# Attention with beacons and a low-rank mixer on one core: two q loads on another queue, a weight quarter ahead of half of v, and small loads issued sooner

## The chip, the core and the metric

The kernel runs on one core of a Trainium2 chip. The metric is the device time of one execution in microseconds (us); lower is better. The core has five engines that run side by side and wait for one another through semaphores: TensorE (PE, matrix products and transposes), VectorE (DVE), ScalarE (ACT), GpSimd (POOL) and SyncE (SP). In the profile PE's weight loads have a line of their own, PEld. DMAs are issued by POOL (the software queue, q0 in the profile; it can convert f32 to f16 on the way) or by SP and ACT (hardware queues, which here move f32 as f32).

## The reference

```python
# q, k, v: (B=8, H=8, S=576, D=64); beacon_k, beacon_v: (8, 8, 16, 64); all f32
k_all, v_all = concat([beacon_k, k]), concat([beacon_v, v])      # 592 keys
scores = q @ k_all.T / 8, causal over the 576 tokens, beacons always seen
x = softmax(scores) @ v_all            # laid out as (B, S, H * D = 512)
h = x.transpose @ U @ V                # U: (576, 32), V: (32, 576)
u = x + h.transpose
out = u + relu(u @ w_ch1) @ w_ch2      # 512 -> 2048 -> 512
```

## The kernel before, in words

Work goes in *pairs*: two heads of one batch at a time, four pairs to a batch, 32 in all. For a pair, PE transposes q and k (`qkT_units`, lines 277 and 283) into PSUM, DVE copies them to `qT` and `kT` (line 310), PE makes the scores (`score_units`, line 350, with the causal mask added on PE at line 342 for pairs 0, 1 and 4), ACT takes the exponentials (line 356), DVE masks them where PE did not (`mask_head`, lines 326 and 328), and PE multiplies by v (`av_unit`, line 399), after which DVE normalises into `xb` (lines 407 and 408). When a batch is done the low-rank product follows (for the first batch `first_mix`: `head` at line 491 needs `Usb`, `rest` at line 508 needs `Vsb`), and then the two large products in blocks of 512 tokens (`mlp_units`, lines 536 and 562), whose units are played between the later pairs' steps. All of it stands in an order written out by hand: each engine executes its own instructions strictly in that order.

The change touches the opening, up to about 20 us, in which batch 0 goes through attention with no large product to lie beside it. Its loads are:

- `load_first` brings q and k of pair 0 (`stq`, `stk`, f32) by SP and ACT. `build_masks` adds q of pair 1 by SP, into the second part of `stq`, and k of pair 1 by POOL. A cell of `stq` is zeroed on DVE first (line 126); the DMA waits for that, which places it behind the memset in time.
- For pairs 2 and 3, POOL loads k and q, converted to f16, into `Ls[0]` (line 205). `by_heads` transposes such a tile head by head, 12 transposes a pair. A pair that came in f32 is first copied to an f16 tile with both heads beside each other (`regroup`, line 270), and `in_pair` then needs 6 transposes.
- v of batch 0 comes in two halves, heads 0 to 3 (`HALVES[0]`) and heads 4 to 7 (`HALVES[1]`), five DMAs each (`v_tokens`, line 220), by POOL. Pairs 0 and 1 use the first half, pairs 2 and 3 the second.
- `emit_w1(i)` loads a quarter of w_ch1 (line 191), by POOL; its first quarter is first used by line 536, after pair 3's products have begun.
- `small_loads` zeroes a cell of its tile on DVE (line 167), issues U and V by SP (lines 169 to 174) and returns `cast`, which rounds them on POOL to `Usb` and `Vsb` (lines 178 and 179) and then spreads copies by SP (lines 183 and 184).

POOL issues its DMAs in order, one after the other, and each takes it some time. PSUM has eight banks, handed out in a fixed rotation (`pst`, `emptying`).

Of the kernel before, what the change touches and what calls it, by code (L numbers as in the profile page):

```python
# [11 lines left out]
F32 = mybir.dt.float32  # L12
# [6 lines left out]
P = 128  # L19
# [11 lines left out]
def kernel(  # L31
# [13 lines left out]
    nc = tc.nc  # L45
    B, H, S, D = q.shape
# [18 lines left out]
    TJ = 6  # L65
# [29 lines left out]
    gtp = ctx.enter_context(tc.tile_pool(name="gtp", bufs=2))  # L95
# [9 lines left out]
    def pst(shape, dtype, name):  # L105

        b = emptied.pop(0)
        t = psum.tile(shape, dtype, tag=f"bank{b}", name=name)
        bank_of[id(t)] = (b, t)
        return t  # L110

    def emptying(t):
        emptied.append(bank_of.pop(id(t))[0])
# [8 lines left out]
    def build_masks():  # L122
        make_identity(nc, ident)
        nc.vector.memset(bigmask[:, 0, P - Nb : P], F16_MAX)
        nc.vector.tensor_copy(out=identb, in_=ident)
        nc.vector.memset(first[1][0:1, 2, 0:1], 0.0)
        token_load(nc.sync, q[0], first[1], SETS[1])
        make_upper_triangular(nc, mask, val=F16_MAX, diag=True)
        token_load(nc.gpsimd, k[0], Ls[0][0][0], SETS[1])
        nc.vector.tensor_copy(out=bigmask[:, 0, 0 : P - Nb], in_=mask[:, Nb:P])  # L130
        nc.vector.tensor_copy(out=bigmask[:, 1, :], in_=mask)
        for i in range(2):
            nc.vector.tensor_scalar(
                out=negmask[:, i, :], in0=bigmask[:, i, :], scalar1=1.0, scalar2=NEG,
                op0=ALU.is_lt, op1=ALU.mult,
            )
        prs[0] = [None, regroup(first, 0, 1, V, act_copy)]
# [26 lines left out]
    def small_loads():  # L164

        f = utp.tile([P, NT * R + S], F32, name="small", tag="ut")
        nc.vector.memset(f[0:1, 0:1], 0.0)
        uf, vf = f[:, 0 : NT * R].rearrange("p (j r) -> p j r", r=R), f[0:R, NT * R :]
        nc.sync.dma_start(out=uf[: nq[0], 0, :], in_=moe_U[0 : nq[0], :])
        nc.sync.dma_start(  # L170
            out=uf[:, 1 : NT - 1, :], in_=moe_U[q0[1] : QM, :].rearrange("(j p) r -> p j r", p=P)
        )
        nc.sync.dma_start(out=uf[:NL, NT - 1, :], in_=moe_U[QM:S, :])
        nc.sync.dma_start(out=vf, in_=moe_V)

        def cast():
            for rr, jj in ((nq[0], slice(0, 1)), (P, slice(1, NT - 1)), (NL, slice(NT - 1, NT))):
                nc.gpsimd.tensor_copy(out=Usb[:rr, jj, :], in_=uf[:rr, jj, :])
            nc.gpsimd.tensor_copy(out=Vsb[0:R, :], in_=vf)
            for cc in range(NCC):  # L180
                rs = ds(R * cc, R)
                if cc:
                    nc.sync.dma_start(out=Vsb[rs, :], in_=Vsb[0:R, :])
                nc.sync.dma_start(out=Vend[rs, cc, :], in_=Vsb[0:R, QM:S])

        return cast

    def emit_w1(i):
        w1r = moe_w_ch1.rearrange("(cc p) f -> p cc f", p=P)
        fs = ds(FF // 4 * i, FF // 4)  # L190
        nc.gpsimd.dma_start(out=w1[:, :, fs], in_=w1r[:, :, fs])
# [9 lines left out]
    def beacon_load(eng, src, dst, hs):  # L201
        eng.dma_start(out=dst[0:Nb], in_=src[hs].rearrange("h p d -> p h d"))  # L202

    def token_load(eng, src, dst, hs):
        eng.dma_start(out=dst[0:TP, hs, :], in_=src[hs].rearrange("h (p j) d -> p h (j d)", j=TJ))  # L205

    def key_beacons(eng, src, dst, hs):
        beacon_load(eng, src, dst[TP:TB, hs, (TJ - 1) * D : TJ * D], hs)

    def by_head(vs):  # L210
        return vs[:, :].rearrange("p (c h e) -> p c h e", h=H, e=E)

    def v_beacon(bsrc, vs):
        beacon_load(nc.gpsimd, bsrc, by_head(vs)[:, 0, :, 0:D], ALLH)

    def v_tokens(src, vs, hs, js=range(NT)):
        dst = by_head(vs)[:, :, hs, 0:D]
        for j in js:
            a = Nb if j == 0 else 0
            nc.gpsimd.dma_start(  # L220
                out=dst[a : a + nq[j], j, :, :], in_=src[hs, ds(q0[j], nq[j]), :].rearrange("h p d -> p h d")
            )
# [5 lines left out]
    def by_token(t):  # L228
        return t.rearrange("p h (j d) -> p j h d", j=TJ)
# [3 lines left out]
    def qk_tiles():  # L233

        t = [stage.tile([P, TJ * DM], F16, name=f"st{i}", tag=f"st{i}") for i in range(2)]
        st = [x[:, :].rearrange("p (h e) -> p h e", h=H) for x in t]
        whole = [x[:, 0 : NT * DM].rearrange("p (j h d) -> p j h d", h=H, d=D) for x in t]
        return st, whole
# [8 lines left out]
    def keep_warm(ps, n, a=ident):  # L247


        w = ps.shape[-1] // P  # L250
        for _ in range(n):
            nc.tensor.matmul(
                ps[:, 0 : w * P].rearrange("p (a b) -> p a b", b=P), a,
                a.rearrange("p (a b) -> p a b", a=1).broadcast_to([P, w, P]),
                start=True, stop=True,
            )

    def idle(n, a):
        ps = pst([P, 512], F32, name="idle")
        keep_warm(ps, n, a)  # L260
        emptying(ps)

    def regroup(st, c, i, *copies, beacons=True):

        t = pairs.tile([P, TJ, 2, D], F16, name=f"pr{i}", tag=f"pr{i}")
        src = by_token(st[i][:, 2 * c : 2 * c + 2, :])
        w = TJ // len(copies)
        for a, copy in enumerate(copies):
            js = slice(w * a, w * (a + 1))
            copy(out=t[0:TP, js], in_=src[0:TP, js])  # L270
        if i == 0 and beacons:
            copies[0](out=t[TP:TB, TJ - 1], in_=src[TP:TB, TJ - 1])
        return t
# [359 lines left out]
    Ls, qTs, xbs = {}, {}, {}  # L633
# [35 lines left out]
    SETS = [slice(2 * c, 2 * c + 2) for c in range(NH2)]  # L669

    first = []

    def load_first():

        kf = gtp.tile([P, 2, TJ * D], F32, name="stk", tag="gT")
        qf = gtp.tile([P, 4, TJ * D], F32, name="stq", tag="gT")
        first.extend([kf, qf])
        for src, dst in ((q[0], qf), (k[0], kf)):
            for eng, h in ((nc.sync, 0), (nc.scalar, 1)):
                token_load(eng, src, dst, slice(h, h + 1))  # L680
        Ls[0] = qk_tiles()
        key_beacons(nc.gpsimd, beacon_k[0], Ls[0][0][0], ALLH)
        nc.scalar.activation(out=warm, in_=ones, func=AF.Exp)

    def act_copy(out, in_):
        nc.scalar.activation(out=out, in_=in_, func=AF.Copy)

    prs = {}
    V = nc.vector.tensor_copy
# [32 lines left out]
    def scores_of(p):  # L722
        b, c = divmod(p, NH2)
        return score_units(c, qTs[b], kTs[b % 2], expts_of(p), p in ON_PE)
# [86 lines left out]

    with tc.manual_schedule(engines={ENG.PE, ENG.Activation, ENG.DVE, ENG.SP, ENG.Pool}):
        load_first()
        build_masks()
        for c in (2, 3):
            for src, dst in zip((k[0], q[0]), Ls[0][0]):
                token_load(nc.gpsimd, src, dst, SETS[c])
            if c == 2:
                v_beacon(beacon_v[0], vss[0])
                v_tokens(v[0], vss[0], HALVES[0])  # L820
        prs[0][0] = regroup(first, 0, 0, V, act_copy, beacons=False)
        idle(IDLE[0], plain)
        t0, sc = qkT_of(0), scores_of(0)
        t0[0]()
        idle(IDLE[4], ident)
        t0[1]()
        sc[0](IDLE[1], gs=[1, 0])
        prs[1] = [None, regroup(first, 1, 1, V)]
        for u in qkT_of(1):
            u()  # L830
        clear()
        cast = small_loads()
        sc[1]([3, 2], False)
        sc = scores_of(1)
        sc[0](IDLE[2])

        v_tokens(v[0], vss[0], HALVES[1])
        emit_w1(0)
        cast()
        Ls[1] = qk_tiles()  # L840
        (kt, qt), _ = Ls[1]
        token_load(nc.gpsimd, k[1], kt, HALVES[0])
        token_load(nc.gpsimd, q[1], qt, HALVES[0])
        key_beacons(nc.gpsimd, beacon_k[1], kt, ALLH)
        emit_w1(1)
        token_load(nc.gpsimd, k[1], kt, HALVES[1])
        token_load(nc.gpsimd, q[1], qt, HALVES[1])
# [7 lines left out]
        for p in range(2):  # L855
            qt, kt = qkT_of(p + 2)
            kt()
            sc[1]([3, 2], False)
            qt()
            av = av_of(p)  # L860
            av[0]()
            mask_head = sc[3]
            sc = scores_of(p + 2)
            if p:
                mask_head(0)
            sc[0](0, av[1])
            if p:
                mask_head(1)
# [122 lines left out]
        for p in range(NP1, NP):  # L991
            b, c = divmod(p, NH2)
# [128 lines left out]
```

## Time and profile before

| | |
|---|---|
| median of 3 runs | 351.5 us (350.47, 351.5, 351.79) |
| profiled execution, its own time | 349.7 us |
| its span in the trace | 348.0 us |
| PE busy | 341.3 us of it |
| DVE, ACT, POOL busy | 189.7, 163.6, 97.8 us |
| POOL's DMA queue | 18.18 MB in 87440 packets |
| hardware queue q1 | 22.84 MB in 58928 packets |
| granted TensorE clock | 0.998 |

A timeline row gives the start in us, the time until the last instruction of the row ends, the engine (a "q" behind it stands for the engine's sequencer, which issues a DMA), the line, the operation, output<-inputs, the count, and in brackets the idle time of the engine before it with what ended it. A row of DMA issues gives the count, the size written, and the us from the start of the issue to the landing.

### The profile page before, as it was taken

What the parts mean: (1) busy time and instruction counts of PE and PEld (TensorE: products, weight loads), DVE (VectorE), ACT (ScalarE), POOL (GpSimd) and SP (SyncE); (2) the same over time, 40 slices, a digit from 0 to 9 for tenths busy, and PEclk for the clock granted to TensorE, in tenths of its full rate; (3) what the DMA queues carried; (4) which work ended last, traced back from release to release, by engine and by line L of the source; (5) the groups of instructions that cost most, each with busy time, mean ns of one, the idle gap of its engine ahead of it and who ended that gap; (6) DMA issues with size and microseconds to landing.
All of it is one profiled execution on the core that took longest, in us unless ns stands there. A gap on an engine that the chain in (4) does not pass through costs nothing.

```text
span 348.0 us, 7791 instructions
## 1 busy us (share of the span) xinstructions
PE 341.3 (98%) x3084; PEld 173.2 (50%) x3084; DVE 189.7 (55%) x493; ACT 163.6 (47%) x358; POOL 97.8 (28%) x137
## 2 busy tenths in 40 slices
PE   8899999999999999999999999999999999999995
PEld 4565565455554455444554445455445444444443
DVE  6676965788875553554465556535655542323311
ACT  6957851578723664167615752494434203202300
POOL 8966714544506457303930130000000000000000
PEclk9999999999999999999999999999999999999999
DMA  9999999999999999991999697713122314013011
GB/s 166 135 186 170 169 200 171 216 148 154 128 142 145 167 133 132 154 213 14 146 139 237 64 117 123 184 38 68 62 75 47 69 62 121 2 60 106 17 66 64
DMA packets 146635, 41.88 MB, mean 120 GB/s; under 512 B 131488, under 2 KB 142080, under 8 KB 146592
## 3 DMA queue, kind: packets, MB, share of 16 engines
q0 software_dynamic: 87440, 18.18, 68.2%
q1 hardware_dynamic: 58928, 22.84, 36.0%
q8 instruction: 26, 0.43, 0.5%
q10 hardware_dynamic: 224, 0.30, 0.2%
q14 instruction: 17, 0.14, 0.1%
HBM read 37.37 MB, written 9.44 MB: 134 GB/s over the span
## 4 chain that ended last, share of the span: by engine, by line
PE 93%; POOL 2%; DMA 2%; issue 1%; DVE 1%; ACT 1%; POOLq 0%
PE gps L536 36%; PE cps L562 35%; PE po L399 8%; PE sps L384 6%; DMA st<-in_q_dram 2%; PE tps L277 1%; PE sps L350 1%; POOL vs L220 1%; PE cph L588 1%; PE qtp L436 1%; POOL st L205 1%; PE tps L283 1%; PE ups L461 1%; PE ups L415 1%; ACT expt L356 0%
## 5 line engine op out<-in xcount | busy, mean ns | idle before, releaser
L536 PE MATMUL gps<-uT,w 128*128 128x512 f16 x576 | 136.0, 379 | 0.1
L562 PE MATMUL cps<-w,gT 128*128 128x512 f16 x560 | 130.9, 379 | 0.0
L390 ACT ACTIVATE expt<-sps 128x496 f16<-128x496 f32 x192 | 82.5, 534 | 71.5 <-PE sps L384 71.5
L549 ACT ACTIVATE gT<-gps 128x512 f16<-128x512 f32 x86 | 50.9, 622 | 78.8 <-PE gps L536 78.6
L536 PEld LDWEIGHTS <-w 128*128 128x128 f16 x576 | 51.8, 98 | 58.0 <-issue 2.4
L562 PEld LDWEIGHTS <-gT 128*128 128x128 f16 x560 | 50.8, 98 | 58.9 <-issue 6.2
L551 DVE TENSOR_SCALAR gT<-gps 128x512 f16<-128x512 f32 x58 | 40.0, 690 | 41.9 <-PE gps L536 40.5
L575 DVE TENSOR_TENSOR ob<-cps,ut 128x512 f32<-128x512 f32 x31 | 21.4, 691 | 48.3 <-PE cps L562 47.5
L220 POOL DMA_DIRECT2D vs<-in_v_dram x50 | 39.6, 810 | 17.1 <-PE gps L536 5.8
L399 PEld LDWEIGHTS <-expt 128*128 128x128 f16 (+1 forms) x960 | 36.2, 98 | 12.7 <-issue 0.8
L399 PE MATMUL po<-vs,expt 128*128 128x65 f16 (+1 forms) x960 | 38.9, 194 | 0.0
L408 DVE TENSOR_TENSOR xb<-po,rec 128x320 f16<-128x320 f32 x64 | 31.5, 492 | 2.2
L326 DVE TENSOR_TENSOR expt<-expt,bigmask 128x512 f16<-128x512 f16 x58 | 24.1, 416 | 6.7 <-ACT expt L390 6.7
L356 ACT ACTIVATE expt<-sps 128x496 f16<-128x496 f32 (+2 forms) x64 | 27.1, 584 | 0.9 <-PE sps L350 0.8
L407 DVE RECIPROCAL rec<-po 128x5 f32<-128x5 f32 x64 | 12.1, 188 | 27.0 <-PE po L399 26.8
L384 PE MATMUL sps<-qT,kT 64*128 64x80 f16 (+4 forms) x288 | 23.3, 281 | 0.1
L202 POOL DMA_DIRECT2D vs<-in_beacon_v_dram x8 | 4.3, 536 | 57.8 <-PE po L399 57.7
L384 PEld LDWEIGHTS <-kT 64*128 64x128 f16 x288 | 9.9, 94 | 18.3 <-issue 14.8
L651 POOL DMA_DIRECT2D st<-in_q_dram x20 | 16.9, 863 | 6.6 <-DMA vs<-in_v_dram 2.7
L651 POOL DMA_DIRECT2D st<-in_k_dram x20 | 17.0, 883 | 3.4 <-DMA st<-in_q_dram 3.4
L448 DVE TENSOR_TENSOR uT<-ups,uT 128x496 f16<-128x496 f32 x24 | 14.5, 667 | 5.0 <-PE ups L461 5.0
L310 DVE COPY qT<-tps 128x576 f16<-128x576 f16 (+1 forms) x16 | 11.8, 736 | 4.6 <-PE tps L283 2.8
(98 smaller groups left out, 161.9 us busy)
## 6 DMA issues: line engine op xcount, KB each, us to landing
out_dram<-ob SPq DMA_DIRECT2D x35, 256.0 KB, 2.3
vs<-in_v_dram POOLq DMA_DIRECT2D x18, 128.0 KB, 6.9
w<-in_moe_w_ch_dram POOLq DMA_DIRECT2D x4, 512.0 KB, 6.1
w<-in_moe_w_ch_dram POOLq DMA_DIRECT2D x2, 1024.0 KB, 13.6
st<-in_k_dram POOLq DMA_DIRECT2D x12, 128.0 KB, 8.6
st<-in_q_dram POOLq DMA_DIRECT2D x12, 128.0 KB, 9.6
st<-in_k_dram POOLq DMA_DIRECT2D x2, 576.0 KB, 13.2
st<-in_q_dram POOLq DMA_DIRECT2D x2, 576.0 KB, 16.1
```

The lines of the kernel that those rows point to most:

```text
L220: nc.gpsimd.dma_start(out=dst[a : a + nq[j], j, :, :], in_=src[hs, ds(q0[j], nq[j]), :].rearrange("h p d -> p h d"))
L326: nc.vector.tensor_tensor(out=e4, in0=e4, in1=bigmask, op=ALU.min)
L356: nc.scalar.activation(out=ex[i][:, ds(SLOT * g, gw[g])], in_=ps[g, i][:, 0 : gw[g]], func=AF.Exp, scale=scale)
L384: nc.tensor.matmul(ps[p, g, i][:, ds(o, w)], kT[hp, c, ds(P * ch, P)], qT[hp, c, ds(qa, w)], start=True, stop=True,)
L390: nc.scalar.activation(out=at[p][3][i][:, ds(SLOT * g, gw[g])], in_=ps[p, g, i][:, 0 : gw[g]], func=AF.Exp, scale=scale)
L399: nc.tensor.matmul(po[:, j, :], ex[0 : nk[c], ds(blk[(c, j)], P)], vs[0 : nk[c], ds(c * H * E + h * E, E)], start=(c == 0), stop=(c == j),)
L408: nc.vector.tensor_tensor(out=xb[:, :, ds(h * D, D)], in0=po[:, :, 0:D], in1=r.broadcast_to([P, NT, D]), op=ALU.mult)
L536: nc.tensor.matmul(g[:, 0:n], w1[:, cc, ts(dc, P)], uT[:, cc, ds(t0, n)], start=(cc == 0), stop=(cc == NCC - 1))
L549: nc.scalar.activation(out=gT["t"][:, dc, 0:n], in_=g[:, 0:n], func=AF.Relu)
L551: nc.vector.tensor_scalar_max(out=gT["t"][:, dc, 0:n], in0=g[:, 0:n], scalar1=0.0)
L562: nc.tensor.matmul(ps[:m, :], gT["t"][:, dc, ds(P * i, m)], w2[:, dc, :], start=(dc == 0), stop=turned and dc == NDC - 1, skip_group_check ...
L651: nc.gpsimd.dma_start(out=dst[a : m[j], j, :, :], in_=src[:, ds(q0[j], nq[j]), :].rearrange("h p d -> p h d"))
```

## The change

- q of pairs 2 and 3 comes by SP, in f32, into `stq`, which grows from four heads to eight. `load_q` zeroes the cells on DVE and issues the loads; for pair 1 this is what was there before, for pairs 2 and 3 it stands behind pair 0's `regroup`. DVE casts each of the two q's to f16 (`regroup`): pair 2's behind `clear()`, pair 3's behind the copy of pair 2's k. Their transposes are the 6 of `in_pair` instead of the 12 of `by_heads`.
- POOL no longer issues these two q loads.
- `small_loads` (U and V by SP) is called behind pair 0's first scores instead of behind `clear()`.
- w_ch1's first quarter is issued ahead of v's second half instead of behind it.
- `cast` stands behind the first k, q and beacon loads of batch 1 instead of ahead of them.

```diff
 def build_masks():
...
-        nc.vector.memset(first[1][0:1, 2, 0:1], 0.0)
-        token_load(nc.sync, q[0], first[1], SETS[1])
+        load_q(1)
...
-        qf = gtp.tile([P, 4, TJ * D], F32, name="stq", tag="gT")
+        qf = gtp.tile([P, H, TJ * D], F32, name="stq", tag="gT")
...
+    def load_q(*cs):
+        for c in cs:
+            nc.vector.memset(first[1][0:1, 2 * c, 0:1], 0.0)
+        for c in cs:
+            token_load(nc.sync, q[0], first[1], SETS[c])
...
         for c in (2, 3):
-            for src, dst in zip((k[0], q[0]), Ls[0][0]):
-                token_load(nc.gpsimd, src, dst, SETS[c])
+            token_load(nc.gpsimd, k[0], Ls[0][0][0], SETS[c])
             if c == 2:
                 v_beacon(beacon_v[0], vss[0])
                 v_tokens(v[0], vss[0], HALVES[0])
         prs[0][0] = regroup(first, 0, 0, V, act_copy, beacons=False)
+        load_q(2, 3)
...
         sc[0](IDLE[1], gs=[1, 0])
+        cast = small_loads()
         prs[1] = [None, regroup(first, 1, 1, V)]
         for u in qkT_of(1):
             u()
         clear()
-        cast = small_loads()
+        prs[2] = [None, regroup(first, 2, 1, V)]
         sc[1]([3, 2], False)
         sc = scores_of(1)
         sc[0](IDLE[2])
 
+        emit_w1(0)
         v_tokens(v[0], vss[0], HALVES[1])
-        emit_w1(0)
-        cast()
         Ls[1] = qk_tiles()
         (kt, qt), _ = Ls[1]
         token_load(nc.gpsimd, k[1], kt, HALVES[0])
         token_load(nc.gpsimd, q[1], qt, HALVES[0])
         key_beacons(nc.gpsimd, beacon_k[1], kt, ALLH)
+        cast()
         emit_w1(1)
...
             kt()
+            if p == 0:
+                prs[3] = [None, regroup(first, 3, 1, V)]
             sc[1]([3, 2], False)
             qt()
```

## The prediction

> **What bounds the kernel now.** The first view is the page's busy times, the second the waits of PE over the whole span.
>
> ```profile
> PE 341.3 (98%) x3084; PEld 173.2 (50%) x3084; DVE 189.7 (55%) x493; ACT 163.6 (47%) x358; POOL 97.8 (28%) x137
> ```
>
> ```profile
> PE sps L350 <- DVE qT L310: 0.6, 2, 0.3
> PE tps L283 <- DMA st<-in_q_dram: 0.4, 1, 0.4
> ```
>
> PE is busy for 341.3 of 348.0 us, and of its few waits only one is for a transfer: a transpose that waits 0.4 us for q. So whatever the change gives or takes must show as PE idle time in the opening, and what PE gains there it keeps only if no later wait takes its place. The third view, the chain that ended last, shows where that wait lies. It is pair 3's q.
>
> ```profile
> 9.82 5.47 DMA st<-in_q_dram
> 15.29 0.04 issue
> 15.34 0.47 PE tps L283 x12
> 15.80 0.02 issue
> 15.82 0.77 DVE qT L310
> 16.59 0.05 issue
> 16.64 0.58 PE sps L350 x4
> 17.22 0.57 PE po L399 x15
> 17.78 0.41 PE sps L350 x8
> 18.19 0.56 PE po L399 x15
> ```
>
> The load is issued at 9.82 and lands at 15.29. PE transposes it, DVE copies it, pair 3's first scores start at 16.64, and from there one piece of PE work follows the other without a gap: pair 1's second head, pair 3's last scores, and at 18.19 the first head of pair 2 times v, which ends at 18.75. The timeline of ACT, the fourth view, shows the same delay from the other side.
>
> ```profile
> 6.88 9.95 ACT L356 ACTIVATE expt<-sps 128x464 f16<-128x464 f32 x24 [0.62 <-PE sps L350]
> 17.05 3.39 ACT L356 ACTIVATE expt<-sps 128x496 f16<-128x496 f32 x8 [0.23 <-PE sps L350]
> ```
>
> Pairs 0 to 2 keep ACT occupied without a break from 6.88 to 16.83; then it stands for 0.23 us until pair 3's scores come. So up to 16.6 ACT sets the pace, and small delays on PE before that are covered. The stage's limit is ACT first, then q's landing, then PE.
>
> **Pair 3's q sooner: -0.44 us.** By SP the load is issued behind DVE's cast of pair 0's k, so soon after 5.35. How long such a load takes is seen in SP's timeline and in the DMA issues: q of pair 1, the same size.
>
> ```profile
> 4.80 0.55 DVE L270 CAST pr<-stk 96x384 f16<-96x384 f32 x1 [0.33 <-DMA stk<-in_k_dram]
> 5.30 0.48 DVE L310 COPY qT<-tps 128x288 f16<-128x288 f16 x1
> 5.87 0.48 DVE L310 COPY kT<-tps 128x288 f16<-128x288 f16 x1
> 6.25 0.54 DVE L270 CAST pr<-stq 96x768 f16<-96x768 f32 x1
> ```
>
> ```profile
> 2.95 0.33 SPq L205 DMA_DIRECT2D stq<-in_q_dram  x1
> ```
>
> ```profile
> stq<-in_q_dram SPq DMA_DIRECT2D x1, 288.0 KB, 3.3
> ```
>
> Pair 2's q lands near 5.4 + 3.3 = 8.7, pair 3's one issue (0.33) later at the earliest, 9.1; if it only starts when pair 2's has landed, it is 5.4 + 6.6 = 12.0 at the latest. PE then no longer waits for it at 15.34 but goes on from its last scores at 15.34 - 0.44 = 14.90. DVE can follow, as its rows show:
>
> ```profile
> 10.20 0.76 DVE L310 COPY kT<-tps 128x576 f16<-128x576 f16 x1 [0.79 <-PE tps L283]
> ```
>
> ```profile
> 11.88 0.76 DVE L310 COPY qT<-tps 128x576 f16<-128x576 f16 x1 [0.85 <-PE tps L283]
> ```
>
> ```profile
> 15.18 0.15 DVE L315 COPY kT<-tps 128x16 f16<-128x16 f16 x1
> ```
>
> It is free of pair 3's k at 15.33, and the transposes end at 14.90 + 0.47 = 15.37: the copy ends 0.44 sooner, and so do pair 3's scores (16.20) and, all else equal, the whole PE sequence; pair 2's v product then runs from 17.75 to 18.31. That the 6 transposes are wider and fewer I count at nothing: 12 take 0.47, so 6 save at most half, and the copy behind them is bound by DVE's 15.33 anyway.
>
> **The two added casts and three memsets: 0.** A cast of one pair's q takes 0.54 (the row at 6.25). Pair 2's stands ahead of the copy at 10.20, before which DVE idles 0.79, and pair 3's ahead of the copy at 11.88, behind 0.85 of idle time: both fit, if q has landed by 10.20 - 0.54 = 9.66 and 11.34. The first has a margin of 1.0 us, the second of 2.2, or, at the late end, a deficit of 0.7. A late one would hold up DVE's copy behind it and PE's scores in turn by as much, but ACT has work queued there. I take 0, with 0 to 0.5 as bounds. A memset of one cell is priced by the one that moves with U and V:
>
> ```profile
> 9.35 0.06 DVE L167 MEMSET small<- 1x1 f32 x1
> ```
>
> Two come ahead of the copy at 5.30, 0.12 at most, and 0.09 of idle time lies between that copy's end, 5.78, and the next at 5.87; the third stands ahead of the cast at 6.25, where ACT has its first scores ahead of it. The first scores shift by 0.1 at most, and I take 0.
>
> **POOL: v's second half behind w_ch1's first quarter: takes back more than it gave.** The rows of POOL's queue, then the issues of v's two last pieces (80 rows each) and of the weight quarter:
>
> ```profile
> 9.82 0.67 POOL L205 DMA_DIRECT2D st<-in_q_dram  x1
> 10.46 3.63 POOL L220 DMA_DIRECT2D vs<-in_v_dram  x5
> 14.01 0.82 POOL L191 DMA_DIRECT2D w<-in_moe_w_ch_dram  x1
> 14.74 0.49 POOL L178 CAST Usb<-small 112x32 f16<-112x32 f32 x2
> ```
>
> ```profile
> 13.37 0.72 POOL L220 DMA_DIRECT2D vs<-in_v_dram  x1
> ```
>
> ```profile
> vs<-in_v_dram POOLq DMA_DIRECT2D x1, 40.0 KB, 4.0
> ```
>
> ```profile
> w<-in_moe_w_ch_dram POOLq DMA_DIRECT2D x1, 512.0 KB, 6.2
> ```
>
> v's last piece lands at 13.37 + 4.0 = 17.4, 1.3 us before the product that starts at 18.19 comes to its last matmul. The weights land at 14.01 + 6.2 = 20.2, and line 536 first reads them at 22.20:
>
> ```profile
> 22.20 1.03 PE L536 MATMUL gps<-uT,w 128*128 128x512 f16 x4
> ```
>
> So the quarter is 2.0 us early already, and bringing it forward gains nothing; but v's second half now stands behind it. The issues on POOL are no hindrance: two q issues of 0.67 go, one of 0.82 comes ahead, so the weights are issued near 9.2 (9.82 less one q issue) and v's second half from about 10.0. It is the transfers that decide, and their rates are in the table by stretches (the last column is GB/s written):
>
> ```profile
> 6.50:7.50 1.00, 1.00 (x16) 0.53 (x18) 0.31 (x2) 0.62 (x2) 1.00 (x2) 1.00 1.20 165
> 15.50:16.50 1.00, 0.84 (x27) 0.65 (x23) 0.68 (x2) 1.00 (x4) 0.87 (x3) 1.00 1.09 75
> 16.50:18.50 2.00, 1.86 (x40) 1.25 (x41) 1.75 (x8) 1.77 (x5) 2.00 (x4) 1.00 1.17 179
> ```
>
> In the first stretch POOL's queue moves k and q of 144 KB (147 kB) each, 0.9 us apiece at 165 GB/s. In the last it moves the weights: 512 KB (524 kB) at 179 is 2.9 us, and the landings say 20.2 - 17.4 = 2.8. Between v and the weights lies a stretch at 75 GB/s, in which 1 - 75/179 = 0.6 us is lost, as the weights had been issued only at 14.01; issued so much sooner, they close it. The Trainium skill, page "DMA: Bandwidth & Descriptors", section "Issuing engines are not separate DMA queues", says that DMAs from SP, ACT and POOL end on the same 16 engines, and that a second issuer saves only issuing time. By that rule alone the two q's would cost the engines what they cost before, and v's last piece would come at 20.2 - 0.6 = 19.6.
>
> Two ends for the landing of v's last piece. Best: the two q's cost POOL's queue nothing where they go now, and the lost 0.6 is won: 17.4 + 2.9 - 1.8 - 0.6 = 17.9. Worst: the same work in all lies ahead of it as lay ahead of the weights' landing, and nothing is won: 20.2. I take the middle, 19.0; neither row is nearer. Pair 2's first product, ready at 17.75, then ends at 19.05 instead of 18.75 before: +0.3 net, the 0.44 included. At the ends it is -0.44 and +1.5.
>
> **v's first half, U and V, `cast`, what follows: 0.** The first half is read from 11.77 on, last by the fifteenth matmul near 12.3:
>
> ```profile
> 11.77 0.63 PE L399 MATMUL po<-vs,expt 128*128 128x65 f16 x15
> ```
>
> ```profile
> 8.55 0.67 POOL L220 DMA_DIRECT2D vs<-in_v_dram  x1
> ```
>
> ```profile
> vs<-in_v_dram POOLq DMA_DIRECT2D x1, 40.0 KB, 2.7
> ```
>
> Its last piece lands at 8.55 + 2.7 = 11.3. Now one q (0.9) less lies ahead of it and two others run beside it: between 10.6 (issued 0.63 sooner) and 11.3 + 0.9 = 12.2, in time at both ends. `cast` took POOL from 14.74; now it stands at about 10.0 + 3.6 + three issues of some 0.65 = 15.6, and is through near 17, as U and V are there; `Usb` is first read behind 18.3. If that cover were gone, each 0.1 of delay would stand on PE. Later loads of batch 1 have two q's less before them in POOL's queue; nothing waited for them.
>
> **Sum.** On the profiled execution of 349.7 (1.7 around its span of 348.0): 349.7 - 0.44 + 0.74 = 350.0, where 0.74 is what pair 2's product loses to v (19.05 against 18.31). The median is 1.8 above it, so 351.8.
>
> **Rivals.** *v arrives in time* (faster). If the second half lands by 18.3, PE keeps its 0.44: 351.5 - 0.4 = 351.1. For it: the hardware load of 288 KB in 3.3 us beside POOL's, and the gap at 75 GB/s. Against: the best end is only 0.4 before that point. Chance 0.18.
>
> *v lands where the weights landed* (slower). At 20.2 pair 2's product ends at 20.25 instead of 18.75: +1.5, 353.0. It costs anything from a landing after 18.7. For it: POOL's queue moves at most 179 GB/s in any of the three stretches, and the bytes ahead of v's last piece are those that lay ahead of the weights. Against: the lost 0.6. Chance 0.18.
>
> *The casts hold up POOL* (slower). If each added DVE cast kept POOL from making descriptors for its 0.54, v would land 1.1 later, at 20.1, and the time would be 351.8 + 1.1 = 352.9. But POOL's issue that lay under the cast of 6.25 to 6.79 is seen in its timeline:
>
> ```profile
> 6.28 0.82 POOL L220 DMA_DIRECT2D vs<-in_v_dram  x1
> ```
>
> It took 0.82, where five of v's second half take 3.63, 0.73 each: 0.1 per cast, not 0.54. The Trainium skill, page "SBUF — State Buffer", section "SBUF: two separate sides", has this as a trap: a DVE operation in a two-port mode, an f32 copy among them, locks POOL out of writing descriptors; this trace shows a sixth of it at most. Chance 0.04.
>
> Something else, as q of pair 3 landing after 11.34 or the first half of v late: 0.04, split evenly by sign. That leaves 0.56 for the forecast, whose own range is 351.2 to 352.4.
>
> **How the numbers follow.** 0.5% is 1.8 us, about what a measurement of this kernel can tell from no change; no case but the worst comes near it. The three runs before span 1.3 us. *Slower by over 0.5%*: 0.4 of the two slower rivals (0.09), half of the rest (0.02), the forecast's tail (0.04): 0.15. *Faster*: 0.05. *Within*: 0.80. The range reaches from 351.1 less half the runs' spread, 350.5, to 353.0 with a little of it, 353.2.
>
> **What would show it.** Right: no wait of pair 3's transpose; pair 3's scores near 16.2 and no gap in ACT at 16.83; then a wait of line 399 on v's DMA near 18, some 0.7 long, and the weights landed near 16. Wrong: no such wait and line 399 ending near 18.3 (the first rival), one of over 1.5 (the second), POOL issues of over 1 us near 9.5 and 11 (the third), or PE idle before 14.
> <<'E' cat >/dev/null

## The result, and the profile after

The change makes the kernel slower. The median of six runs is 353.65 us (352.39 to 354.21) against 351.08 us (350.47 to 351.79) for six runs of the kernel before beside them: a ratio of 1.007, 95% interval 1.0043 to 1.0096. Of all the runs told of below a single one counts as slow, 358.12 us in a kernel with idle matmuls, and it is not in that kernel's ratio. The profiled execution took 352.39 us with a span of 350.6 us, where before it was 349.7 and 348.0; its granted clock was 1.0 throughout. Lines of the kernel after stand one lower here: 398 is the product with v (399 before), 349 the scores (350), 535 the first large product (536).

PE's busy time grew by 0.8 us. The waits of PE over the whole span show the rest (us in total, times, longest):

```profile
PE 342.1 (98%) x3072; PEld 173.4 (49%) x3072; DVE 191.3 (55%) x497; ACT 163.7 (47%) x358; POOL 96.4 (28%) x135
```

```profile
PE po L398 <- DMA vs<-in_v_dram: 1.7, 3, 0.9
PE sps L349 <- ACT expt L355: 0.5, 1, 0.5
```

Pair 3's wait for q is gone. In its place PE waits three times for v, 1.7 us in all. PE's timeline says where:

```profile
12.51 0.43 PE L398 MATMUL po<-vs,expt 128*128 128x65 f16 x9
13.85 0.31 PE L398 MATMUL po<-vs,expt 128*128 128x65 f16 x5 [0.90 <-DMA vs<-in_v_dram]
14.65 0.19 PE L398 MATMUL po<-vs,expt 80*128 80x65 f16 x1 [0.49 <-DMA vs<-in_v_dram]
16.73 0.43 PE L276 MATMUL tps<-ident,pr 96*128 96x96 f16 x6
18.13 0.58 PE L349 MATMUL sps<-qT,kT 64*128 64x496 f16 x4 [0.52 <-ACT expt L355]
20.35 0.54 PE L398 MATMUL po<-vs,expt 128*128 128x65 f16 x6 [0.27 <-DMA vs<-in_v_dram]
24.34 1.03 PE L535 MATMUL gps<-uT,w 128*128 128x512 f16 x4
```

Two of the three waits are in the first head of pair 0, for the *first* half of v: one of its pieces comes when nine matmuls of the product have long been done, the last when fourteen are. Only the third, 0.27, is for the second half, the one that the change moved behind the weights. Pair 3's transposes at 16.73 wait for nothing, but they are 1.4 us later than before (15.34). The first large product starts at 24.34 instead of 22.20. From there on PE's work stands 2.07 to 2.14 us later, to the end; so nothing that matters happens behind the opening. (The span grew by 2.6; the last 0.5 lies behind the last instruction of an engine.)

The chain that ended last, which began its part here with pair 3's q before, now runs through v:

```profile
4.92 2.96 POOL vs L219 x4
7.88 6.72 DMA vs<-in_v_dram
14.60 0.04 issue
14.65 0.19 PE po L398
...
20.23 0.33 DVE expt L325
20.56 0.12 DVE expt L327
20.68 0.01 issue
20.70 0.19 PE po L398
```

The last piece of the first half is issued at 7.88 and lands at 14.60: 6.72 us, where it took 2.7 before. The second part of the chain says something of the wait at 20.35, too: the product's last matmul, at 20.70, is released by DVE's mask, which ends at 20.68. So v's second half, whose last piece landed at 20.65, and a mask that is late because of the first half come together; take one away and the other stays.

ACT shows the cost to it, one row for its work up to pair 0's product and one from there on:

```profile
7.67 6.67 ACT L355 ACTIVATE expt<-sps 128x464 f16<-128x464 f32 x16 [0.71 <-PE sps L349]
15.19 6.75 ACT L355 ACTIVATE expt<-sps 128x496 f16<-128x496 f32 x16 [0.85 <-PE sps L349]
```

Before, 24 exponentials stood in one row without a break. Now ACT stands for 0.85 us after the sixteenth, since the next scores stand behind the waiting product in PE's order.

Why v is late shows in the DMA queues. First the stretch from 9 to 10 us of the kernel before, then that of the kernel after (packets, MB, share of 16 engines; transfers under way together may exceed 100%):

```profile
q0 software_dynamic: 932, 0.12, 182.2%
```

```profile
q1 hardware_dynamic: 140, 0.21, 95.5%
q0 software_dynamic: 93, 0.01, 18.4%
```

POOL's queue moved 932 packets of v in that us before, of 128 bytes each. With the two q's of the hardware queue under way it moved 93, against 140 of the hardware queue, which are of 1.5 KB. The bytes go some 18 to 1 to the queue with the large packets (140 x 1.5 KB against 93 x 128 bytes).

One thing in this pair of traces is not due to the change. The first exponential starts at 6.88 before and 7.67 after. In all 14 traces of this case that start lies between 6.79 and 7.67, without order by kernel: 7.09 in a second trace of the kernel after, 7.57 in the fastest kernel of all. What it hangs on isn't shown: in that fastest kernel the loads of pair 0 landed as early as in the kernel before.

### The profile page after: what moved, and what is told of

It reads as the page before. It is cut to its first block, busy times and chain, and to the rows that moved or that the text cites. A ratio compares the mean times of both kernels' runs of the same rounds, so it can differ in the third digit from the quotient of the medians.

```text
span 350.6 us, 7772 instructions
## 1 busy us (share of the span) xinstructions
PE 342.1 (98%) x3072; PEld 173.4 (49%) x3072; DVE 191.3 (55%) x497; ACT 163.7 (47%) x358; POOL 96.4 (28%) x135
## 4 chain that ended last, share of the span: by engine, by line
PE 92%; DMA 2%; DVE 2%; POOL 2%; issue 1%; ACT 1%; POOLq 0%
PE gps L535 36%; PE cps L561 35%; PE po L398 8%; PE sps L383 6%; DMA vs<-in_v_dram 2%; PE tps L276 1%; PE cph L587 1%; PE sps L349 1%; POOL vs L219 1%; PE qtp L435 1%; PE ups L460 1%; PE tps L282 1%; PE ups L414 1%; ACT expt L355 0%; DVE xb L407 0%
```

## The experiments

The runs come in three groups, each with the kernel before beside it: its medians are 350.65 (23 runs), 351.06 (30) and 350.53 us (29). Ratios are to the runs of the kernel before in the same group, with 95% intervals. The clock of a run is its mean granted TensorE clock; since it turns out to differ between kernels, it is given.

The first theory: v's first half is late because two hardware loads run beside it, and the rest of the change adds little. The rival is the prediction's own: v's second half behind the weights. The first group takes the change apart.

**Only the q's by SP** (with their casts; weights and U, V as before).

```diff
-            for src, dst in zip((k[0], q[0]), Ls[0][0]):
-                token_load(nc.gpsimd, src, dst, SETS[c])
+            token_load(nc.gpsimd, k[0], Ls[0][0][0], SETS[c])
...
+        load_q(2, 3)
...
+        prs[2] = [None, regroup(first, 2, 1, V)]
...
+                prs[3] = [None, regroup(first, 3, 1, V)]
```

> The kernel before with only the two q loads moved to SP (their casts with them); U, V, cast and the weight quarter stay where they were. Crowding theory (the two hardware loads take the DMA engines from POOL's queue while v's first half is due): v's first half lands 2 to 3 us later than the 11.3 of before, PE waits for it in line 398 for 0.5 to 1.2 us, ACT has a gap near 14.5, and the time is 1.0 to 2.0 us over before, most of the change's +2.1. Weights theory (v's second half behind the quarter is what costs): no such wait, pair 3's scores 0.4 sooner, 0.2 to 0.5 us under before.

Measured: 352.48 us (12 runs), ratio 1.0047 (1.0023 to 1.0071). Its waits, and ACT's row behind the wait:

```profile
PE po L398 <- DMA vs<-in_v_dram: 1.6, 3, 0.8
```

```profile
15.32 1.98 ACT L355 ACTIVATE expt<-sps 128x496 f16<-128x496 f32 x4 [1.58 <-PE sps L349]
```

All three waits are in pair 0's first head, as with the whole change; none is for the second half. So this part by itself makes the kernel slower. Its trace has one thing more, in the table by stretches (PEclk is the column behind the busy times):

```profile
14.40:17.80 3.40, 3.40 (x45) 2.04 (x42) 1.80 (x5) 2.15 (x5) 1.84 (x6) 0.50 1.37 120
```

For 3.4 us, from the end of the waits on, PE was granted half its clock. Of the 12 runs six had a mean clock under 0.997 and took 353.1 us on average; the other six took 351.6. So about 1 us of this part's loss is there at the full clock too, and the lower clock goes with another 1.5 us where it comes.

**Only the weights' quarter ahead of v's second half.**

```diff
-        v_tokens(v[0], vss[0], HALVES[1])
         emit_w1(0)
+        v_tokens(v[0], vss[0], HALVES[1])
```

> The kernel before with only w_ch1's first quarter issued ahead of v's second half. Weights theory: v's last piece lands near 19.6 to 20.2 instead of 17.4 and pair 2's product ends 0.9 to 1.5 us later; time 0.9 to 1.5 us over before. Crowding theory: it has no say on this part of the opening by itself; what the edit costs here is a part of the change's +2.1 only if v's second half is still what PE waits for last there.

Measured: 355.69 us (353.21 to 358.27, 6 runs), ratio 1.0127 (1.008 to 1.0175), the slowest kernel of all and far over the 0.9 to 1.5 us that were expected; all its runs had clocks of 0.985 to 0.995.

```profile
PE po L399 <- DMA vs<-in_v_dram: 2.3, 3, 2.0
```

```profile
7.22 13.22 ACT L356 ACTIVATE expt<-sps 128x464 f16<-128x464 f32 x32 [0.71 <-PE sps L350]
```

```profile
19.60:23.00 3.40, 2.66 (x24) 1.74 (x25) 0.75 (x3) 0.84 (x3) 3.40 (x7) 0.51 0.78 84
23.00:30.00 7.00, 7.00 (x70) 4.75 (x69) 3.29 (x11) 1.26 (x3) 4.65 (x7) 0.51 1.29 202
```

ACT works through all four pairs without a break, so the first half was in time; v's second half landed between 19.86 and 21.47, PE waited 2.3 us for it, and from 19.7 on, near the end of the longest wait, it had half its clock for 10.2 us. The weights had landed at 19.47, 9.0 us after their issue where they took 6.2 before; no q runs by SP beside them in this kernel, so what held them up is open. The waits alone do not make up 5 us; the clock must carry much of the rest, which a later kernel tries.

**Only U and V sooner, rounded later.**

```diff
         sc[0](IDLE[1], gs=[1, 0])
+        cast = small_loads()
...
         clear()
-        cast = small_loads()
...
         emit_w1(0)
-        cast()
...
         key_beacons(nc.gpsimd, beacon_k[1], kt, ALLH)
+        cast()
```

> The kernel before with only U and V issued behind pair 0's first scores and their cast on POOL behind the two loads and the beacons of batch 1. Crowding theory: the 576 small packets of U run beside v's first half instead of pair 3's q: v's first half up to 0.5 later, pair 3's q up to 1 us sooner; time between 0.4 under and 0.3 over before. Weights theory: within 0.2 of before.

Measured: 350.00 us (12 runs), ratio 0.9982 (0.9964 to 0.9999): the fastest kernel of the study, ahead of both. Pair 3's q, still by POOL, landed at 14.48 instead of 15.29, and ACT's row has no gap:

```profile
7.57 13.22 ACT L356 ACTIVATE expt<-sps 128x464 f16<-128x464 f32 x32 [1.02 <-PE sps L350]
```

The wait for q that the two new loads were to remove is gone here without them. v's first half came later, its last piece at 12.38, and still in time. That U and V beside the q had made the wait is not shown, though. In two other kernels, which leave U and V where they were, PE doesn't wait for pair 3's q either: with only the weights ahead it landed at 15.03 and PE came to it at 15.16; with only two casts added (further below) it landed at 14.77, just ahead of PE:

```profile
14.81 0.45 PE L283 MATMUL tps<-ident,st 96*64 96x96 f16 x12
```

So the wait that the prediction started from stood in one execution and not in others.

**The kernel after once more**, on the chip of these three.

> The changed kernel once more, for its start: its first exponential stood at 7.67 us where that of before stood at 6.88, with the loads of pair 0 landing 0.2 to 0.6 later though issued at the same time. If that is the chance of one execution, the first exponential here is anywhere from 6.8 to 7.7 and the time still 1.5 to 2.9 us over before; if the change causes it, it is at 7.5 or later again.

Measured: 353.67 us (6 runs), ratio 1.0082 (1.0051 to 1.0114). This trace began at 7.09.

```profile
PE po L398 <- DMA vs<-in_v_dram: 2.3, 4, 0.8
```

Two waits of the four, 1.40 together, are again in pair 0's first head; the other two, 0.86 together, are for the second half. The first large product is 2.40 us late. So the loss doesn't come from the late start of the first trace.

Three terms are now on the table: the first half beside the hardware loads, the second half behind the weights, and the clock. The second group separates them.

**The kernel after with the weights behind v's second half again.**

```diff
-        emit_w1(0)
         v_tokens(v[0], vss[0], HALVES[1])
+        emit_w1(0)
```

> The changed kernel with w_ch1's first quarter behind v's second half again. If the change loses twice, once by v's first half and once by v's second, the second wait (0.3 to 0.8 of line 398 near 20.5) goes, pair 2's product ends 1.2 to 1.5 sooner, and the time is 0.6 to 1.4 us over before instead of 3.0. If the hardware loads alone are the cause, the time stays within 0.5 of the changed kernel's.

Measured: 353.14 us (10 runs), ratio 1.0064 (1.0041 to 1.0088). The second half landed at 18.49 and no product waited for it; all 2.8 us of waits for v are in pair 0's first head, where its last piece came at 15.95. (This trace is of an execution of 354.76 us; nine of the ten runs had a clock under 0.997.)

```profile
PE po L398 <- DMA vs<-in_v_dram: 2.8, 3, 1.1
```

Taking the weights' move out of the change gives back no amount that these runs can tell from nothing, though that move alone cost 1.27%. That agrees with the chain of the kernel after, in which pair 2's product is late anyway when the first half is.

**The kernel after, with idle matmuls in the waits**: three short groups on a constant tile ahead of pair 0's product, two ahead of pair 2's. Only the clock can gain by it.

```diff
+            idle(3 if p == 0 else 0, ident)
             av[0]()
...
+        idle(2, ident)
         av[0]()
```

> The changed kernel with three idle matmuls (about 0.38 each, results unused) ahead of pair 0's product with v and two ahead of pair 2's, where PE stands waiting for v. If the lower granted clock of most runs follows from PE's standing still, it stays at 0.997 or more in all runs and the median falls from 353.7 to 352.0 to 352.8, although PE has more to do. If the clock falls for another reason, the time is the same or up to 1 us longer, with clocks of 0.99 as before.

Measured: 352.96 us (12 runs), ratio 1.0051 (1.0032 to 1.0069). Of its 12 runs, 10 had a clock of 0.997 or more; of the 12 of the kernel after in two groups, 4. Those 4 average 352.6 us, the other 8 354.0. The expectation (all runs, at most 352.8 us) was just missed. The interval of the ratio overlaps that of the kernel after, so the gain by itself is not shown; the change in the clocks is. In the profiled execution it was another load that came late, pair 1's q, by 1.5 us, so this trace says nothing on v.

**The kernel before, with the two loads added and nobody using them** (pairs 2 and 3 still take their q from POOL's loads).

```diff
+        load_q(2, 3)
         idle(IDLE[0], plain)
```

> The kernel before with the two hardware loads of q added and not used: the q's still come by POOL, and there are no casts on DVE. Crowding theory: the loads alone make v's first half late (landing at 13.5 to 15 instead of 11.3), PE waits for it 1 to 2 us, time 1.5 to 3.5 over before. If instead the casts on DVE or their place cost the time in the change, no such wait and within 0.5 of before.

Measured: 353.9 us (7 runs), ratio 1.0085 (1.0058 to 1.0113); the clock was 0.999 in the profile and 0.988 to 0.993 in five of the seven runs. PE's rows of pair 0's product:

```profile
12.33 0.50 PE L399 MATMUL po<-vs,expt 128*128 128x65 f16 x5
13.07 0.28 PE L399 MATMUL po<-vs,expt 128*128 128x65 f16 x4 [0.24 <-DMA vs<-in_v_dram]
13.72 0.49 PE L399 MATMUL po<-vs,expt 128*128 128x65 f16 x6 [0.37 <-DMA vs<-in_v_dram]
```

v's first half now is late without any other part of the change: its last piece landed at 13.98.

```profile
vs<-in_v_dram POOLq DMA_DIRECT2D x1, 40.0 KB, 5.5
```

Issued at 8.48, it took 5.5 us. In the four traces with neither the two loads nor an earlier U and V (the kernel before, only the weights without and with idle matmuls, only the casts) it landed between 11.27 and 11.53; with only the q's by SP at 14.51. That the loads delay it is shown. The time is not a clean price of that, since only 0.6 us of PE's waits are for v here, less than the 1 to 2 expected; a wait of 1.5 us far behind the opening (at 62 us, for a later batch's transposes) is in this trace as well.

**Only the weights ahead, with five idle matmul groups in the wait.**

```diff
+        idle(5, ident)
         av[0]()
```

> The kernel before with the weight quarter ahead of v's second half, and five idle matmuls (about 1.9 us) in the place where PE waits 2.0 us for v. If the long wait lowers PE's clock, and that is where most of the 5 us came from, the clock is back at 0.997 or more and the time falls from 355.7 to 353.0 to 354.2: the 2.5 to 3.0 us of the late landing stay. If the landing alone costs the 5 us, the time stays at 355 or more.

Measured: 353.38 us (12 runs), ratio 1.0048 (1.0029 to 1.0067), clocks of 0.997 or more in 10 of 12 runs, where the same kernel without idle matmuls had none in 6. (The run of 358.12 us had 0.985.) The two intervals don't meet: some (1.0127 - 1.0048) x 351 = 2.8 us of what the weights' move cost was the clock; by the ends of the intervals it may be anything from 0.5 to 5 us. What is left, 0.0048 x 351 = 1.7 us, is no more than the 2.3 us of waits for v without the idle matmuls.

The third group asks whether any q can go by SP without harm, and prices the casts.

**U and V sooner, and pair 3's q alone by SP, issued late**, where U and V were issued before.

```diff
         clear()
-        cast = small_loads()
+        load_q(3)
```

> U and V sooner and cast later as in the changed kernel, the weight quarter behind v, and of the two q's only pair 3's by SP, issued behind the masks' copies near 9.5 to 10, when all of v's first half has been issued and most of it moved. Crowding theory: it is the moment that costs, not SP's queue: v's first half lands by 12.9, PE does not wait for it or under 0.2, and the time is within 0.5 of the kernel with U and V sooner alone, 0.2 to 0.9 under before. If a hardware load of q costs whenever it runs: 1 us or more over before.

Measured: 353.64 us (6 runs), ratio 1.0084 (1.0053 to 1.0116), clocks of 0.988 to 0.996 in all six runs; the expectation missed. v's first half came in time (12.44), but now pair 3's k was late, landing at 14.61 (13.75 with U and V alone moved), and q itself landed at 14.92, 5.0 us after its issue at 9.96.

```profile
PE sps L350 <- DVE xb L408: 1.0, 1, 1.0
PE tps L283 <- DMA st<-in_k_dram: 0.5, 1, 0.5
```

I had put the cast ahead of pair 0's normalisation in DVE's order, and so the wait for q reached pair 0: the first row. So the time isn't the price of the load alone, and the clock has its part in it: it stood at a half for 3.4 us behind that wait. The second row would fit a load that, moved away from v, holds up what POOL's queue then has under way. It doesn't show it: with the weights ahead and idle matmuls, where no q runs by SP, pair 3's k landed as late, at 14.54.

**Only pair 2's q by SP.**

```diff
-            for src, dst in zip((k[0], q[0]), Ls[0][0]):
+            for src, dst in tuple(zip((k[0], q[0]), Ls[0][0]))[: c - 1]:
...
+        load_q(2)
...
+        prs[2] = [None, regroup(first, 2, 1, V)]
```

> The kernel before with only pair 2's q moved to SP (issued near 5.6) and its cast; pair 3's q stays on POOL. Half the crowding: v's first half lands at 12.0 to 13.2 instead of 11.3 (13.5 to 16 with both), PE waits 0 to 0.6 for it, time between 0.2 under and 0.9 over before, clocks mostly 0.997 or more. If the cost does not go with the bytes that run beside v, it is that of both q's, 1.7 over.

Measured: 351.41 us (12 runs), ratio 1.0029 (1.0003 to 1.0056), all clocks 0.997 or more. v's last piece landed at 12.84: one load delays it by 1.5 us, two by 2.7 (unused) and 3.2 (only the q's). PE did not wait for it, and the clock stayed. Why 0.3% is lost all the same its trace, of an execution of 353.96 us, doesn't settle; 1.5 us of waits stand at a later batch's transposes, as in the kernel with the unused loads, and I can't say if that is the loads' doing.

**Only the casts**: the kernel before, with two more f32 to f16 casts on DVE in the two places, of pair 1's q, unused.

```diff
         clear()
+        regroup(first, 1, 1, V)
...
+            if p == 0:
+                regroup(first, 1, 1, V)
```

> The kernel before with the two added DVE casts alone, on data that is there already and with results unused. By the prediction's sum 0, within 0.3 of before; by its third rival each holds up POOL's descriptors by 0.5 and the time is 0.5 to 1.5 over.

Measured: 350.97 us (10 runs), ratio 1.0012 (0.999 to 1.0033). No cost is shown. A POOL issue that lay under the first cast:

```profile
9.13 0.83 POOL L205 DMA_DIRECT2D st<-in_k_dram  x1
```

It took 0.83, where such an issue took 0.64 to 0.67 elsewhere; the second cast lay over issues of v that took 0.74 each (four in 2.96), as before.

**Only U and V sooner, rounded in the old place.**

```diff
+        cast = small_loads()
         prs[1] = [None, regroup(first, 1, 1, V)]
...
         clear()
-        cast = small_loads()
```

> The kernel before with U and V issued sooner, their cast on POOL where it was. If it is the small packets of U beside pair 3's q that made the wait of before, pair 3's q lands near 14.5 as with the cast later too, no wait for it, and the time is 0.3 to 0.8 under before. If the later cast gave the gain, by letting batch 1's loads go first, the time is that of before within 0.3.

Measured: 350.39 us (12 runs), ratio 0.9993 (0.9978 to 1.0009). PE did not wait for pair 3's q here either (its landing isn't in this trace); the gain is too small to be told from none, and from that of the version with the rounding moved. So neither of the two explanations is decided.

## Why the prediction was wrong, by its steps

**Pair 3's q sooner, -0.44: right on the load, without worth.** The two q's were issued at 5.96 and 6.33 and landed at 10.38 and 11.76, inside the bounds of 8.7 to 12.0. The transpose waits no more. But PE comes to it 1.4 us later than before, so there is no gain left, and the gap of ACT that I took for a sign of pair 3's q reappears, longer, at 15.19. The 0.44 itself was read from one execution. With only the casts PE didn't wait for this q, and its first large product started at 21.78 instead of 22.20, by about the 0.44; yet its last products started only 0.04 us ahead of those of the kernel before, and both spans are 348.0 us. So even where the wait was absent, nothing of it was kept to the end.

**The casts and memsets, 0: right** (1.0012, interval across 1). Pair 2's q landed 0.7 later than the 9.66 that its place on DVE allowed, and DVE stood 0.32 us for it; ACT's queued work covered that, as the prediction said. The rival that the casts hold POOL for their whole length is gone: an issue took 0.83 in place of 0.65, which is 0.18 more and not 0.54.

**v's second half behind the weights, +0.74: the right wait, sized too small.** I had its landing between 17.9 and 20.2 and took 19.0. The wait that I put near 18, 0.7 long, came at 20.35 with 0.27, since the first half had delayed PE by then. The weights landed at 17.34 (near 16 was expected), v behind them at 20.65 with the whole change, and 21.47 with this part alone, beyond the end that I called the worst. That end assumed that the same work takes POOL's queue the same time in another order; with this part alone the weights took 9.0 us from issue to landing instead of 6.2, and why stays open. With the whole change there is one link more, on POOL itself, whose issues I had called no hindrance:

```profile
12.43 1.49 POOL L219 DMA_DIRECT2D vs<-in_v_dram  x2 [1.06 <-DMA vs<-in_v_dram]
```

POOL stands for a landing of v before it issues the second half's third piece. Such waits between the issues of v's second half, of 0.3 to 1.5 us, are in all six traces that have both q's beside v's first half, and in none of the other eight. So the second half is late in part because the first is: with the loads unused it landed at 19.16 instead of 17.37, with the weights behind it as before. For the part alone the prediction was right that PE waits (2.3 us of waits), and wrong in size, by the landing and by the clock.

**v's first half, 0: the step that failed.** I wrote that it lands between 10.6 and 12.2, "in time at both ends", and named PE idle before 14 as the sign of being wrong; that is the sign that came. It landed at 14.60 and, with the weights behind, at 15.95. The upper end gave the two q's the price of one of POOL's q's, 0.9 us, as if bytes shared the engines. The rows of the queues speak for packets. I counted them in ten stretches of 1 us in which a q of the hardware queue ran beside v, between 7.5 and 10.5 us: two each in the two traces of the kernel after, in that with only the q's, with the weights behind, and with the loads unused. The first of them (kernel after, 7.5 to 8.5) and the last (loads unused, 9.5 to 10.5):

```profile
q1 hardware_dynamic: 185, 0.27, 82.6%
q0 software_dynamic: 194, 0.02, 37.7%
```

```profile
q1 hardware_dynamic: 146, 0.22, 88.0%
q0 software_dynamic: 240, 0.03, 47.4%
```

The hardware queue moved 121 to 185 packets in them, mean 157, POOL's queue 114 to 361, mean 218; alone POOL's queue moved 932 in the us shown above. One q is 288 KB in packets of 1.5 KB, 192 of them; two take 384/157 = 2.4 us. In that time v gets 2.4 x 218 = 520 packets rather than 2.4 x 932 = 2240, and the 1720 that are left need 1.8 us at 932 per us afterwards. The kernel with the loads unused, which issues v as before, shows 2.7; the rest of it I haven't split. With the whole change the delay was 3.3 us (14.60 against 11.3) with an issue 0.6 sooner; there U's and V's loads run beside v as well, which delay the last piece by 1.1 us alone (12.38 with only U and V sooner).

A rival would be that the hardware queue simply goes first. The kernel with only U and V sooner speaks against it. From 8.5 to 9.5 us its hardware queue moves U, in packets of 128 bytes like v's:

```profile
q0 software_dynamic: 738, 0.09, 143.7%
q1 hardware_dynamic: 389, 0.05, 50.6%
```

POOL's queue still moved 738 packets, where it moved 927 in that us of the kernel before. U has fewer bytes than a q, so this does not separate packets from bytes.

The Trainium skill, page "DMA: Bandwidth & Descriptors", section "Queues, rings and completion order", says that each DMA engine goes round among the queues that have work, a packet at a time; a packet there is typically 9 to 17 descriptors. Whether the packets that the profile counts, of 128 bytes and of 1.5 KB, are packets in that sense no trace here says. Their counts, 157 against 218 in the mean, are not far from one for one, though single stretches lie between 121 against 361 and 179 against 114; and near one for one the bytes are unequal wherever one queue's packets are twelve times the other's. I had weighed another section of this page of the Trainium skill, that issuers share the 16 engines, against the bytes in all; it says nothing of whose bytes come first. That packets are the measure is thus argued from counts and not shown. A trial with q in smaller packets would be the direct test, and wasn't made.

**The missing rival: the clock.** The prediction priced a wait of PE at its own length. In several kernels it cost more, since the granted clock fell to a half in it or just behind it: 3.4 us long with only the q's, 10.2 with only the weights. Idle matmuls in the same wait took some 2.8 us of the loss with only the weights away. With the whole change the two runs in three with a lower clock took some 1.3 us more (354.0 against 352.6). The length of the waits doesn't decide it alone: the two traces of the kernel after have 1.7 and 2.3 us of them at a clock of 1.0. The Trainium skill, page "TensorE: Matmul & The Clock Gate", section "Part 1: The HAM clock gate (the "warmup" mystery)", has the clock set by PE's activity in windows of 4096 cycles, about 3.4 us, that run free of the kernel. The stretches here, 3.4 and three times 3.4, agree, and so does it that one kernel falls into it in some executions and not in others.

**U and V sooner, 0: near.** It is the one part of the change that gains, if anything: 0.9982 with the rounding behind the loads of batch 1, 0.9993 with it where it was.

So the loss of 2.6 us in the medians is: v's first half late, which sets pair 2's product too (with only the q's: 1.0047, 1.6 us); the clock behind such waits in most executions; and of the weights' move little that is visible inside the whole change (1.0064 without it against 1.007 and 1.0082), though it costs 1.27% alone. The costs of the parts don't add up, for they are waits in a row on the same engine. What of the difference between 1.0047 and 1.007 is the weights' and what is chance stays open.

The lowest time of the study is the kernel before with U and V sooner and rounded later. In it the wait that the prediction started from, pair 3's q, is gone without any hardware load of q; whether that is the doing of U and V is open, since it is absent with only the casts as well.

## What to carry to other kernels

Before a load is moved to another queue, look at what the queue it leaves has under way at that time, and compare the sizes of the packets and not the bytes alone: beside v's packets of 128 bytes, q's of 1.5 KB took the larger part of the engines until q was done. A load that frees 0.4 us and lands beside one that is due within 1 us is a bad trade. And where PE is the bound, waits of some 2 us can cost about as much again through the clock (some 2.8 us beside waits of 2.3 here); compare the granted clock of all runs, not of the profiled one, and try a few idle matmuls in the wait.

## What the runs showed of the hardware that I had not expected

- POOL's queue fell from 932 packets in a us to 93 while the hardware queue moved 140 packets of 1.5 KB.
- A q of 288 KB by SP took 3.3 us ahead of v (2.95 to 6.21, kernel before), 4.4 and 5.4 us beside v in the kernel after, up to 6.6 with only the q's, and 5.0 beside POOL's k of pair 3.
- Half the clock was granted for 3.4, 6.8 and 10.2 us in or just behind waits of PE of 1.6, 2.8 and 2.3 us in all, while 1.7 and 2.3 us left it at 1.0 in the two traces of the kernel after. The mean clock was under 0.997 in every run of two kernels (only the weights, and pair 3's q late), in 8 of 12 of the kernel after and in 5 of 82 of the kernel before.
- POOL stood 0.3 to 1.5 us before issuing more of v, between the issues of its second half, in all six traces with both q's beside the first half and in no other.
- The start of the first exponential varies by 0.9 us from execution to execution, with no order by kernel.
